# Memory at the border of two loops laid anew, and the backward loop's loads issued by GpSimd

## The chip, the core and the metric

The kernel runs on one core of a Trainium2 chip. A core has five engines that run their own instruction streams: TensorE (PE, matrix products), VectorE (DVE), ScalarE (ACT), GpSimd (POOL) and SyncE (SP), which here only issues transfers. Transfers between device memory (HBM) and the on-chip memory (SBUF), and transposes on the way, are carried out by 16 DMA engines; an instruction on SP or POOL starts them. Results of matrix products land in PSUM. The metric is the device time of one execution in microseconds (us); the time before is 1559.46 us, the median of 3 runs (1558.28 to 1564.76).

## The reference

The program is the forward and the backward pass of one transformer layer with its two branches in parallel, in bf16, for one sequence of S = 2048 rows of D = 448, with 16 heads of 28 and a feed-forward width of 1792:

```python
x  = A_x                                   # [1, 2048, 448]
xn = (x - mean(x)) / sqrt(var(x) + 1e-5)
q, k, v = split(xn @ wqkv)                 # 16 heads, Dh = 28
p   = softmax(q @ k.T * Dh ** -0.5)
mha = concat_heads(p @ v) @ wo
ffn = (silu(xn @ w_gate) * (xn @ w_up)) @ w_down
out = x + mha + ffn
# results: out, and for grad_out (the gradient of out) the gradients of
# x, wqkv, wo, w_gate, w_up, w_down
```

## The kernel before, in words

A head's 28 columns are padded to 32, so four heads make a group of 128 partitions (G = 4 groups, `g`) and two heads a pair (8 pairs, `pr`). The order of instructions on each engine is the order in which the program writes them. There is no planner; waits come from the tiles that the instructions share, and from pools: a tile of a pool with n buffers waits for the readers and writers of the tile n before it, and a pool opened after others are closed waits for whatever was last done in the memory that it gets.

*Prologue (0 to about 60 us).* x is loaded and normalized, the weights of the projections are padded into `wq_sb`, Q, K and V of group 0 are made.

*Forward attention loop (to about 680 us).* It runs over steps (g, qc, kt): 4 groups, 4 blocks of 512 query rows, 16 tiles of 128 keys. A step makes the scores of four heads (L651), their exponentials (L655), and the product with V (L628, `pv`). Between these matmuls PE takes items from a queue: `fill(pace)` pops so many items as the work left, spread over the steps left, allows. The items are the whole feed-forward branch, forward and backward, tile of F by tile of F (`ffn_items`, L432 to L489: its matmuls write to `f_ps`, its temporaries come from the pool `ftmp`), the weight gradients of that branch (`dW_items`, L401: `dwd_sb` and `dw_o` are their output tiles, `dw_o` written by a transpose that SP issues, L425), the projections of the next group, and for each finished block of 512 rows the attention output and its gradient (`o_items`, from L527: tiles `o_raw`, `rlc`, `oT`, `dOl`, `dOT` from the pools `op_` and `op1`). `o_items` stores the gradient in two forms: `spo_d` (rows, L581) and `dOT_d` (transposed, L585), and SP stores the hidden activations and their gradients in `hO_d`, `da_d`, `du_d`. The last items of the loop are those of the last block (`late`): the transposes `tr`, the products `do`, then 16 matmuls and a copy for the gradient of wo (`dwo_items`, L514) and its store to out_3 by four GpSimd instructions (`dwo_out`, L509).

*The border (about 680 to 692 us).* The pools of the forward loop are closed, those of the backward loop opened (`wp` for weights, `ckp` for chunks, `spg` for row forms, `ework` for E, `dwork` for ds, `twin` for dsT). SP issues the loads of Ksp (a transpose), dOsp (from `spo_d`), the four pieces of W_down and two chunks.

*Backward loop (to about 1485 us).* 512 units, each a pair, a block of 512 keys (`kc`), and 128 query rows (`w`, `qi`). A unit makes scores (L959) and the gradient of the probabilities (L969) on PE, E by ScalarE's exponential (L978), and ds by VectorE's multiply (L984). Eight units make a window W (64 windows). A window's ds are needed transposed: three transfers of two units each (dsT, 512 KB, SP, L1011), the last two units by PE and VectorE (L894, L896). From E and ds come the gradients of V and K (`acc_mm`, L868, with dOsp and Qsp), from dsT that of Q (`dq_mm`, L909, with Ksp). `dq_out` (L913) sums the latter on GpSimd over the key blocks; `dkv_sp` and `dq_sp` are transposes of finished gradients which SP issues two or three units later (`sp_later`). Every window also carries one filler job on PE: W 1 to 16 the output rows (`y`, L823: 19 matmuls, with W_down, `wo_pad` and x), later the gradients of wqkv (`dwq`) and dx from da (W 22 to 37) and from du (W 42 to 49 and 54 to 61), 14 or 15 matmuls each (L829). The job of a window takes a chunk `ck` (576 or 448 KB) and often an `x_c` (112 KB), which `job_load` (L736) loads two windows ahead into pools with three buffers. `extra_load` (L711) issues, one a window, the pieces of the next pair (QD and KV, L594 to L600), the rows of the next group (Qsp and Ksp by transposes, dOsp by a load, L602 to L610), the weights W of the next stage (L709) and, in the last two windows, grad_out (`dy`, L728). The results of the jobs leave by GpSimd's stores from `row_o`.

All these loads and transposes of the backward loop are issued by SP, so they share SP's instruction stream and one DMA queue (q1). GpSimd's transfers have another queue (q0). Window 0 calls `job_load(2)` twice: once ahead of the loop, and once as W + 2.

*Final loop (about 1504 us to the end).* 16 row tiles of dx: partial sums and the gradients of Q, K, V times the weights of wqkv (L1037 on), the backward pass of the norm, the store.

Of the kernel before, what the change touches and what calls it, by code (L numbers as in the profile page):

```python
# [38 lines left out]
def kernel(  # L39
# [52 lines left out]

# [7 lines left out]
    wq_sb = bp.tile([P, 4, 3, G, P], BF16, name="wq_sb")  # L100
# [4 lines left out]
    op_ = bst.enter_context(tc.tile_pool(name="op_", bufs=2))  # L105
    op1 = bst.enter_context(tc.tile_pool(name="op1", bufs=1))
# [294 lines left out]
    def dW_items(fc):  # L401

        out = []
        for wi in range(3):
            box = {}

            def go(t, wi=wi, box=box):
# [9 lines left out]
                if wi == 0:  # L417
                    o = fpool["ftmp"].tile([P, D], BF16, name="dwd_sb")
                    dve.tensor_copy(out=o[:], in_=acc[:, :D])
                    pool.dma_start(out=out_6[fc * P:(fc + 1) * P, :], in_=o[:])  # L420
                else:
                    w = dwT[wi - 1]
                    dve.tensor_copy(out=w[:, :D], in_=acc[:, :D])
                    o = fpool["ftmp"].tile([P, 4, P], BF16, name="dw_o")
# [89 lines left out]
    def dwo_items(g):  # L514
        box = {}

        def go(t):
# [3 lines left out]
            if t == NT - 1:  # L521
                o = fpool["ftmp"].tile([P, D], BF16, name="dwd_sb")
                dve.tensor_copy(out=o[:], in_=box["ps"][:, :D])
                dwo_out(g, o)
        return [[(MMD, lambda t=t: go(t)) for t in range(NT)]]

    def o_items(g, qc, o_ps):  # L527

        o_raw = op_.tile([P, 512], FP32, name="o_raw")
# [6 lines left out]
        def tr(i):  # L536
# [8 lines left out]
            rlc = st["rlc"] = op_.tile([P, 4, 4], FP32, name="rlc")  # L545
# [5 lines left out]
            oT = op_.tile([P, 512], BF16, name="oT")  # L551
# [5 lines left out]
        def do(i):  # L557
# [5 lines left out]
            if i < 3:  # L563
# [3 lines left out]
            prod = op1.tile([P, 16, HP], FP32, name="prod")  # L567
            dve.tensor_tensor(out=prod[:], in0=dps,
                              in1=O_sp[g][:, tsl, :].rearrange("p t (h r) -> p (t h) r", r=HP), op=ALU.mult)
            delta = op_.tile([P, 16], FP32, name="delta")  # L570
            dve.tensor_reduce(out=delta[:], in_=prod[:, :, 0:DH], axis=AX.X, op=ALU.add)
            dOl = op_.tile([P, 4, P], BF16, name="dOl")
            dOv = dOl[:].rearrange("p t (h r) -> p (t h) r", r=HP)
            dve.tensor_tensor(out=dOv, in0=dps, in1=rlb.unsqueeze(2).to_broadcast([P, 16, HP]), op=ALU.mult)
            ndl = op_.tile([P, 16], FP32, name="ndl")
            dve.scalar_tensor_tensor(out=ndl[:], in0=delta[:], scalar=-1.0, in1=rlb, op0=ALU.mult, op1=ALU.mult)
            dve.tensor_copy(out=dOv[:, :, 28], in_=ndl[:])
            lo = op_.tile([P, 16], FP32, name="lo")
# [3 lines left out]
            dT = op_.tile([P, 512], BF16, name="dOT")  # L582
# [5 lines left out]
                    + (dwo_items(g) if qc == 3 else []))  # L588


# [3 lines left out]
    def load_pair(pr, pieces=range(4)):  # L594
# [3 lines left out]
        for i in pieces:  # L598
            sp.dma_start(out=qd[pr][i % 2][64 * (i // 2):64 * (i // 2) + 64],
                           in_=(qT_d, kT_d, dOT_d, vT_d)[i][g, r:r + 64, :])  # L600

    def load_rows(g, i):  # L602
# [3 lines left out]
        if i == 2:  # L606
            sp.dma_start(out=t[:].rearrange("p t c -> p (t c)"), in_=spo_d[g])
# [26 lines left out]
    for i, (g, qc, kt) in enumerate(steps):  # L634
# [45 lines left out]
    wp = cst.enter_context(tc.tile_pool(name="wp", bufs=2))  # L680
# [18 lines left out]
    wtile, chunk, dsp, dqacc = {}, {}, {}, {}  # L699

    w_src = {"wd": B_w_down.rearrange("(fc p) d -> p fc d", p=P), "wg": wT_d[0], "wu": wT_d[1], "wq": wqT_d}

    def load_w(nm, pieces=range(4)):
        if 0 in pieces:
            wtile[nm] = wp.tile([P, NFC, D], BF16, name="W")
        for i in pieces:
            sl = slice(4 * i, min(4 * i + 4, 3 * G if nm == "wq" else NFC))
            if sl.start < sl.stop:
                sp.dma_start(out=wtile[nm][:, sl], in_=w_src[nm][:, sl])  # L709
# [14 lines left out]
    def load_dy(i):  # L724

        if i == 0:
            wtile["dy"] = wp.tile([P, NFC, D], BF16, name="W")
        sp.dma_start(out=wtile["dy"][:, 7 * i:7 * i + 7], in_=dy_d[:, 7 * i:7 * i + 7, :])  # L728
# [7 lines left out]
    def job_load(i):  # L736
# [3 lines left out]
        if j[0] == "y":  # L740
            t = ckp.tile([P, NFC + G, P], BF16, name="ck")
            sp.dma_start(out=t[:], in_=hO_d[j[1]])
            x = ckp.tile([P, D], BF16, name="x_c")
            sp.dma_start(out=x[:], in_=x_d[:, j[1], :])
            chunk[i] = (t, x)
        elif j[0] == "dx":
            t = ckp.tile([P, NFC + G, P], BF16, name="ck")
            sp.dma_start(out=t[:, :NFC], in_=(da_d, du_d)[j[1]][j[2]])
# [378 lines left out]
```

## Time and profile before

| what | value |
|---|---|
| runs | 1558.28, 1559.46, 1564.76 us |
| profiled execution | 1558.67 us |
| span of its instructions | 1556.9 us |
| mean granted TensorE clock | 0.965 of full speed |

By stage (busy us of each engine; DMA is the mean busy share of the 16 DMA engines; GB/s is what they moved):

| stage, us | PE | DVE | ACT | POOL | DMA | GB/s |
|---|---|---|---|---|---|---|
| prologue, 0 to 60 | 43.1 | 38.7 | 31.2 | 18.8 | 0.51 | 132 |
| forward, 60 to 640 | 565.7 | 360.1 | 475.4 | 79.0 | 0.70 | 146 |
| end of forward and border, 640 to 691.9 | 40.6 | 15.3 | 26.9 | 10.6 | 0.52 | 126 |
| backward loop, 691.9 to 1484.7 | 727.4 | 680.0 | 589.6 | 165.9 | 1.11 | 209 |
| between the loops, 1484.7 to 1503.6 | 4.8 | 1.3 | 1.9 | 7.7 | 0.86 | 212 |
| final loop, 1503.6 to 1556.9 | 46.5 | 26.3 | 23.3 | 11.4 | 0.49 | 165 |

How the lines of the profile are read. The page gives first each engine's busy time, its share of the span and its instructions, then the span in 40 slices with a digit for each (9: busy 90% or more). Part 4 follows the chain of work that ended last from the end back to the start, and gives shares of the span by engine and line. Part 5 has one row for each group of instructions: line, engine, operation, output <- inputs with partitions x elements and type, count | busy time in us, mean ns of one | idle time of the engine just ahead of them, and the releaser that ended most of it, with its part. A row of stretches is: from:to in us, its length, the busy time and count of the chosen instructions, granted clock, DMA share, GB/s. A row of a timeline is: start, duration in us, engine, line, operation, output <- input, count, and in brackets the idle time before it with what ended it. SPq and POOLq are the streams of SP and GpSimd; the duration of a transfer there is the time that its issue took, not the transfer's. A row of DMA issues gives the count and the median time from issue to landing.

### The profile page before, as it was taken

What the parts mean: (1) busy time and instruction counts of PE and PEld (TensorE: products, weight loads), DVE (VectorE), ACT (ScalarE), POOL (GpSimd) and SP (SyncE); (2) the same over time, 40 slices, a digit from 0 to 9 for tenths busy, and PEclk for the clock granted to TensorE, in tenths of its full rate; (3) what the DMA queues carried; (4) which work ended last, traced back from release to release, by engine and by line L of the source; (5) the groups of instructions that cost most, each with busy time, mean ns of one, the idle gap of its engine ahead of it and who ended that gap; (6) DMA issues with size and microseconds to landing.
All of it is one profiled execution on the core that took longest, in us unless ns stands there. A gap on an engine that the chain in (4) does not pass through costs nothing.

```text
span 1556.9 us, 31518 instructions
## 1 busy us (share of the span) xinstructions
PE 1428.1 (92%) x12278; PEld 577.4 (37%) x12278; DVE 1121.8 (72%) x1459; ACT 1148.4 (74%) x1312; POOL 293.3 (19%) x479
## 2 busy tenths in 40 slices
PE   6899999999999999969989899889898889999968
PEld 3233333333333333323333335333334333533434
DVE  7465656665666666538977789888888888998935
ACT  4678888887888877647767677777777777787824
POOL 4001111111111111110221122212212222221222
PEclk8899999999999999979999999999999999999979
DMA  6566647766777678769999999999999999999984
GB/s 172 111 151 132 145 101 162 144 147 127 156 151 148 140 152 155 153 176 212 230 214 205 217 195 192 218 205 224 205 204 194 205 226 208 189 212 213 185 224 134
DMA packets 764854, 277.69 MB, mean 178 GB/s; under 512 B 730960, under 2 KB 744208, under 8 KB 764704
## 3 DMA queue, kind: packets, MB, share of 16 engines
q1 hardware_dynamic: 748944, 238.90, 79.8%
q0 software_dynamic: 14960, 36.60, 8.8%
q8 instruction: 96, 1.57, 0.4%
q14 instruction: 54, 0.44, 0.1%
q10 hardware_dynamic: 800, 0.17, 0.1%
HBM read 64.15 MB, written 59.24 MB: 79 GB/s over the span
## 4 chain that ended last, share of the span: by engine, by line
PE 65%; DMA 15%; DVE 9%; ACT 6%; issue 4%; SPq 1%; DVEq 0%; POOL 0%; ACTq 0%; POOLq 0%
DMA dsT<-ds 12%; PE s_ps L651 9%; PE f_ps L413 8%; PE f_ps L439 8%; PE sd L959 6%; PE acc L868 5%; ACT E L978 5%; PE o_ps L628 5%; DVE ds L984 4%; PE aux L909 3%; PE sd L969 3%; PE sd L894 3%; PE f_ps L198 3%; PE sd L1043 2%; PE aux L823 2%
## 5 line engine op out<-in xcount | busy, mean ns | idle before, releaser
L984 DVE TENSOR_TENSOR ds<-sd,E 128x1024 bf16<-128x1024 f32 x512 | 607.8, 1220 | 121.7 <-DMA dsT<-ds 48.0
L978 ACT ACTIVATE E<-sd 128x1024 bf16<-128x1024 f32 x512 | 521.0, 1024 | 194.3 <-PE sd L969 125.1
L655 ACT ACTIVATE eT<-s_ps 128x1024 bf16<-128x1024 f32 x512 | 496.5, 1021 | 135.3 <-PE s_ps L651 134.3
L959 PE MATMUL sd<-KV,QD 32*128 32x512 bf16 x1024 | 203.0, 391 | 47.0 <-DVE ds L984 33.0
L969 PE MATMUL sd<-KV,QD 32*128 32x512 bf16 x1024 | 203.7, 390 | 12.9 <-ACT E L978 4.6
L651 PE MATMUL s_ps<-qT,kT 32*128 32x512 bf16 x1024 | 195.9, 391 | 0.5 <-ACT eT L655 0.5
L868 PE MATMUL acc<-E,dOsp 128*32 128x512 bf16 x1024 | 138.5, 394 | 0.1
L868 PE MATMUL acc<-ds,Qsp 128*32 128x512 bf16 x1024 | 138.5, 394 | 0.0
L959 PEld LDWEIGHTS <-QD 32*128 32x128 bf16 x1024 | 57.6, 91 | 208.2 <-issue 194.5
L439 PE MATMUL f_ps<-xnT,wgu 128*128 128x512 bf16 x448 | 119.5, 385 | 9.6 <-DVE w_sb L465 9.6
L829 PE MATMUL aux<-W,ck 128*128 128x448 bf16 x448 | 112.5, 356 | 0.0
L628 PE MATMUL o_ps<-eT,v_sp 128*32 128x512 bf16 x1024 | 103.6, 397 | 4.9 <-DMA v_sp<-vT 4.9
L651 PEld LDWEIGHTS <-kT 32*128 32x128 bf16 x1024 | 47.1, 91 | 161.4 <-issue 157.9
L413 PE MATMUL f_ps<-xn_sp,f_sp 128*128 128x448 bf16 x448 | 98.9, 354 | 0.0
L969 PEld LDWEIGHTS <-QD 32*128 32x128 bf16 x1024 | 69.1, 91 | 64.1 <-issue 60.3
L894 PE MATMUL sd<-ident_bf,ds 128*128 128x128 bf16 x1024 | 70.8, 224 | 15.7 <-DVE ds L984 15.5
L896 DVE COPY dsT<-sd 128x1024 bf16<-128x1024 bf16 x128 | 82.1, 683 | 3.7 <-PE sd L894 3.5
L413 PEld LDWEIGHTS <-f_sp 128*128 128x128 bf16 x672 | 58.9, 98 | 67.0 <-issue 20.5
L909 PE MATMUL aux<-dsT,Ksp 128*32 128x512 bf16 x1024 | 71.8, 400 | 4.8 <-DMA dsT<-ds 4.8
L894 PEld LDWEIGHTS <-ds 128*128 128x128 bf16 x1024 | 62.4, 100 | 30.5 <-issue 30.4
L451 DVE SCALAR_TENSOR_TENSOR g<-t_sb,f_ps 128x512 f32<-128x512 f32 x56 | 38.4, 685 | 43.8 <-ACT t_sb L449 43.8
L925 POOL TENSOR_TENSOR dq_acc<-dq_acc,dq_s 128x512 f32<-128x512 f32 x32 | 40.5, 1265 | 130.5 <-ACT dq_s L921 130.5
(145 smaller groups left out, 1711.3 us busy)
## 6 DMA issues: line engine op xcount, KB each, us to landing
ck<-hO_d SPq DMA_DIRECT2D x17, 576.0 KB, 5.2
hO_d<-hduT SPq DMA_DIRECT2D x56, 128.0 KB, 3.4
da_d<-hduT SPq DMA_DIRECT2D x56, 128.0 KB, 3.1
du_d<-hduT SPq DMA_DIRECT2D x56, 128.0 KB, 3.3
ck<-da_d SPq DMA_DIRECT2D x16, 448.0 KB, 4.3
ck<-du_d SPq DMA_DIRECT2D x16, 448.0 KB, 4.4
dq_c<-dqkv_d SPq DMA_DIRECT2D x8, 768.0 KB, 5.0
dqkv_d<-dkv_o POOLq DMA_DIRECT2D x64, 64.0 KB, 4.1
```

The source lines that it names most:

```text
L413: pe.matmul(acc[:, :D], lhsT=src[:, t, wi, :], rhs=rhs[:, t, :D], start=(t == 0), stop=(t == NT - 1))
L439: pe.matmul(st[name][:], lhsT=w(c), rhs=src[:, tsl, c, :], start=(c == 0), stop=(c == 3))
L628: pe.matmul(o_ps[HP * hh:HP * (hh + 1), :], lhsT=v[:, kt, HP * hh:HP * (hh + 1)], rhs=e[hh // 2][:, hh % 2, :], start=(kt == 0), stop=(kt ...
L651: pe.matmul(s_ps[:, j, :], lhsT=kT[r:r + HP, kt * P:(kt + 1) * P], rhs=qT[r:r + HP, qc * 512:(qc + 1) * 512], start=True, stop=True, tile_ ...
L655: act.activation(out=e[:], in_=s_ps[:], func=ACT.Exp, scale=SCALE)
L868: pe.matmul(acc[r:r + HP, :], lhsT=src[:, qt, 64 * hp + HP * j:64 * hp + HP * j + HP], rhs=m[:, j, :], start=(qt == 0), stop=(qt == NT - 1 ...
L894: pe.transpose(ps[:, u, i, :], ds[:, u, i // 4, (i % 4) * P:(i % 4 + 1) * P], ident_bf[:])
L909: pe.matmul(ps[r:r + HP, :], lhsT=Ks[:, kc * 4 + kt, 64 * hp + HP * j:64 * hp + HP * j + HP], rhs=dsT[:, 4 * s_:4 * s_ + 4, j, kt, :], sta ...
L959: pe.matmul(s_ps[:, j, :], lhsT=q[HP * j:HP * j + HP, qt * P:(qt + 1) * P], rhs=kv[HP * j:HP * j + HP, kc * 512:(kc + 1) * 512], start=Tru ...
L969: pe.matmul(d_ps[:, j, :], lhsT=q[r:r + HP, qt * P:(qt + 1) * P], rhs=kv[r:r + HP, kc * 512:(kc + 1) * 512], start=True, stop=True, tile_p ...
L978: act.activation(out=E[k][:], in_=s_ps[:], func=ACT.Exp, scale=SCALE)
L984: dve.tensor_tensor(out=ds[:, u % 2], in0=d_ps[:], in1=E[u][:], op=ALU.mult)
```

## The change

It has two halves. The first is about memory and the end of the forward loop:

- `wq_sb` moves from the forward loop's pool `bp` into a new pool `wpa`, which stays open; the backward loop's W_down (`wd`), `wu` and `dy` take its place there one after the other, `wg` and `wq` go to another pool, `wpb`.
- The four loads of W_down are issued by SP during the forward loop, in the last block of the last group at kt = 4, 7, 10 and 13.
- The pools `op_` and `op1` and a new one, `fout` (for `dwd_sb` and `dw_o`, which were in `ftmp`), are opened after `ftmp`; in the backward loop `ework` and `dwork` are opened first. E and ds thereby lie on other memory of the forward loop.
- In the last block, 5 of the matmuls for wo's gradient come ahead of `tr` and `do`, the other 11 after them.
- The loads ahead of the backward loop (Ksp, dOsp, chunk 2) are issued inside its first window: dOsp after unit 2, chunk 2 after unit 4, Ksp after unit 6. The second `job_load(2)` is dropped. In the final loop a pool is opened ahead of two others.

The second half: every load of the backward loop that isn't a transpose (`ck`, `x_c`, W, the pieces of QD and KV for pairs 1 to 7, dOsp, `dy`) is issued by GpSimd instead of SP. The transposes (dsT, Qsp, Ksp, `dkv_sp`, `dq_sp`) stay with SP, and so do the pieces of pair 0 and W_down in the forward loop. SP's instructions fall from 847 to 702, GpSimd's rise from 424 to 549; the order of PE's, DVE's and ACT's is otherwise the same.

```diff
@@ prologue @@
+    wpa = ctx.enter_context(tc.tile_pool(name="wpa", bufs=1))
+    wq_sb = wpa.tile([P, NFC, D], BF16, name="W")[:].rearrange("p n d -> p (n d)")[:, :12 * G * P].rearrange(
+        "p (c t g r) -> p c t g r", c=4, t=3, g=G)
-    wq_sb = bp.tile([P, 4, 3, G, P], BF16, name="wq_sb")
-    op_ = bst.enter_context(tc.tile_pool(name="op_", bufs=2))
-    op1 = bst.enter_context(tc.tile_pool(name="op1", bufs=1))
@@ open_ffn @@
-        for nm, n in (("ftmp", 2), ("fT", 2), ("spp", 2)):
+        for nm, n in (("fT", 2), ("spp", 2), ("ftmp", 2), ("fout", 2), ("op_", 2), ("op1", 1)):
@@ dW_items, dwo_items (dwd_sb, dw_o); o_items (its tiles from fpool["op_"], fpool["op1"]) @@
-                    o = fpool["ftmp"].tile([P, D], BF16, name="dwd_sb")
+                    o = fpool["fout"].tile([P, D], BF16, name="dwd_sb")
...
@@ end of o_items @@
+        if g == G - 1 and qc == 3:
+            a, b, w = late.pop()
+            late.append([w[:5], a, b, w[5:]])
@@ load_w, moved ahead of the forward loop @@
+    wtile = {}
+    w_home = {"wd": wpa, "wu": wpa, "dy": wpa}
...
-                sp.dma_start(out=wtile[nm][:, sl], in_=w_src[nm][:, sl])
+                (sp if nm == "wd" else pool).dma_start(out=wtile[nm][:, sl], in_=w_src[nm][:, sl])
@@ load_pair, load_rows @@
-            sp.dma_start(out=qd[pr][i % 2][64 * (i // 2):64 * (i // 2) + 64],
+            (pool if pr else sp).dma_start(out=qd[pr][i % 2][64 * (i // 2):64 * (i // 2) + 64],
...
-            sp.dma_start(out=t[:].rearrange("p t c -> p (t c)"), in_=spo_d[g])
+            pool.dma_start(out=t[:].rearrange("p t c -> p (t c)"), in_=spo_d[g])
@@ forward loop @@
+        if g == G - 1 and qc == 3 and kt in (4, 7, 10, 13):
+            load_w("wd", [(kt - 4) // 3])
@@ pools of the backward loop @@
-    wp = cst.enter_context(tc.tile_pool(name="wp", bufs=2))
+    wpb = cst.enter_context(tc.tile_pool(name="wpb", bufs=1))
...
-    ckp = ast.enter_context(tc.tile_pool(name="ckp", bufs=3))
-    spg_.append(ast.enter_context(tc.tile_pool(name="spg", bufs=2)))
     ework = ast.enter_context(tc.tile_pool(name="ework", bufs=9))
     dwork = ast.enter_context(tc.tile_pool(name="dwork", bufs=5))
+    ckp = ast.enter_context(tc.tile_pool(name="ckp", bufs=3))
     twin = ast.enter_context(tc.tile_pool(name="twin", bufs=2))
+    spg_.append(ast.enter_context(tc.tile_pool(name="spg", bufs=2)))
...
+    w_home["wg"] = w_home["wq"] = wpb
@@ load_dy, job_load (twice so) @@
-        sp.dma_start(out=wtile["dy"][:, 7 * i:7 * i + 7], in_=dy_d[:, 7 * i:7 * i + 7, :])
+        pool.dma_start(out=wtile["dy"][:, 7 * i:7 * i + 7], in_=dy_d[:, 7 * i:7 * i + 7, :])
...
-            sp.dma_start(out=t[:], in_=hO_d[j[1]])
+            pool.dma_start(out=t[:], in_=hO_d[j[1]])
...
-            sp.dma_start(out=x[:], in_=x_d[:, j[1], :])
+            pool.dma_start(out=x[:], in_=x_d[:, j[1], :])
@@ ahead of and in the backward loop @@
-    load_rows(0, 1)
-    load_rows(0, 2)
-    load_w("wd")
     job_load(1)
-    job_load(2)
...
-            if pos == 0:
+            if pos == 0 and W:
                 job_load(W + 2)
...
+        if k == 2:
+            load_rows(0, 2)
+        if k == 4:
+            job_load(2)
+        if k == 6:
+            load_rows(0, 1)
@@ final loop @@
+        one = fin.enter_context(tc.tile_pool(name="one", bufs=1))
         ckf = fin.enter_context(tc.tile_pool(name="ckf", bufs=4))
         wk = fin.enter_context(tc.tile_pool(name="wk", bufs=3))
-        one = fin.enter_context(tc.tile_pool(name="one", bufs=1))
```

More of the change, by code (lines that the diff above doesn't have):

```diff
@@ L423, in go @@
                     dve.tensor_copy(out=w[:, :D], in_=acc[:, :D])
-                    o = fpool["ftmp"].tile([P, 4, P], BF16, name="dw_o")
+                    o = fpool["fout"].tile([P, 4, P], BF16, name="dw_o")
                     sp.dma_start_transpose(out=o[:], in_=w[:])
@@ L521, in go @@
             if t == NT - 1:
-                o = fpool["ftmp"].tile([P, D], BF16, name="dwd_sb")
+                o = fpool["fout"].tile([P, D], BF16, name="dwd_sb")
                 dve.tensor_copy(out=o[:], in_=box["ps"][:, :D])
@@ L581, in do @@
             pool.dma_start(out=spo_d[g, :, 4 * qc * P:(4 * qc + 4) * P], in_=dOl[:].rearrange("p t c -> p (t c)"))
-            dT = op_.tile([P, 512], BF16, name="dOT")
+            dT = fpool["op_"].tile([P, 512], BF16, name="dOT")
             sp.dma_start_transpose(out=dT[:].rearrange("p (t s) -> p t s", t=4),
@@ L588, in o_items, with load_w @@
                     + (dwo_items(g) if qc == 3 else []))
+        if g == G - 1 and qc == 3:
[3 more added lines that the diff above has]
+    w_home = {"wd": wpa, "wu": wpa, "dy": wpa}
+    w_src = {"wd": B_w_down.rearrange("(fc p) d -> p fc d", p=P), "wg": wT_d[0], "wu": wT_d[1], "wq": wqT_d}
+    def load_w(nm, pieces=range(4)):
+        if 0 in pieces:
+            wtile[nm] = w_home[nm].tile([P, NFC, D], BF16, name="W")
+        for i in pieces:
+            sl = slice(4 * i, min(4 * i + 4, 3 * G if nm == "wq" else NFC))
+            if sl.start < sl.stop:
+                (sp if nm == "wd" else pool).dma_start(out=wtile[nm][:, sl], in_=w_src[nm][:, sl])
     NPR = 2 * G
@@ L698 @@
     NW = N // UW
[L699 to L709, printed above, removed]
+    w_home["wg"] = w_home["wq"] = wpb
+    chunk, dsp, dqacc = {}, {}, {}
     def extra_load(W):
```

22 lines of the change are left out of this document (11 added, 11 removed).

## The prediction

> **What bounds the kernel now.** I read the page first (busy shares, slices, chain, groups), then the unit loop in stretches, then SP's timeline in a crowded and in a quiet stretch, the border between the two loops, and the one place where GpSimd already issues loads beside a transpose. The page:
>
> ```profile
> PE 1428.1 (92%) x12278; PEld 577.4 (37%) x12278; DVE 1121.8 (72%) x1459; ACT 1148.4 (74%) x1312; POOL 293.3 (19%) x479
> ...
> DVE  7465656665666666538977789888888888998935
> ...
> DMA  6566647766777678769999999999999999999984
> ...
> PE 65%; DMA 15%; DVE 9%; ACT 6%; issue 4%; SPq 1%; DVEq 0%; POOL 0%; ACTq 0%; POOLq 0%
> DMA dsT<-ds 12%; PE s_ps L651 9%; PE f_ps L413 8%; PE f_ps L439 8%; PE sd L959 6%; PE acc L868 5%; ACT E L978 5%; PE o_ps L628 5%; DVE ds L984 4%; PE aux L909 3%; PE sd L969 3%; PE sd L894 3%; PE f_ps L198 3%; PE sd L1043 2%; PE aux L823 2%
> ...
> L984 DVE TENSOR_TENSOR ds<-sd,E 128x1024 bf16<-128x1024 f32 x512 | 607.8, 1220 | 121.7 <-DMA dsT<-ds 48.0
> ```
>
> From slice 18 on (the backward loop) the DMA digits are all 9 and the chain goes through the dsT transposes: the multiply of L984 waits 48.0 us for them. One row per stretch of that loop, counting L984 alone (us, DVE busy, count); each begins at the first multiply of a window of 8 units:
>
> ```profile
> 703.70:775.80 72.10, 58.06 (x49) 0.99 1.11 222
> 775.80:834.60 58.80, 38.08 (x32) 0.91 1.09 210
> ...
> 1181.90:1299.80 117.90, 85.09 (x74) 0.96 1.14 214
> 1299.80:1402.80 103.00, 85.59 (x73) 1.00 1.11 200
> ```
>
> A window takes 103.0 / 9 = 11.45 us where nothing is late, 72.1 / 6 = 12.0 in the y stage (19 instead of some 15 matmuls of filler), but 58.8 / 4 = 14.7 in windows 7 to 10 and 117.9 / 9 = 13.1 in 39 to 47. With 17 windows at 11.97 and 47 at 11.45 the loop would take 741.6; from the first multiply (691.94) to the end of the last it takes 792.8. So 51 us are lateness, in the stretches where loads are thick. SP's timeline in such a stretch, and in a quiet one:
>
> ```profile
> 881.45 0.53 SPq L742 DMA_DIRECT2D ck<-hO_d  x1
> 882.07 0.38 SPq L744 DMA_DIRECT2D x_c<-in_A_x_dram  x1
> 882.56 3.89 SPq L1011 DMA_TRANSPOSE dsT<-ds  x1
> 886.50 0.57 SPq L709 DMA_DIRECT2D W<-wT_d  x1
> 887.16 3.36 SPq L1011 DMA_TRANSPOSE dsT<-ds  x1
> ```
> ```profile
> 1452.03 10.49 SPq L1011 DMA_TRANSPOSE dsT<-ds  x4
> ```
>
> SP is busy issuing without a rest in the first; a dsT costs it 10.49 / 4 = 2.62 us undisturbed, 3.4 to 3.9 behind a load. The border:
>
> ```profile
> 683.87 0.54 POOL L585 DMA_DIRECT2D dOT_d<-dOT  x1 [3.58 <-DMA dOT<-dOl]
> 684.40 2.03 POOL L512 DMA_DIRECT2D out_dram<-dwd_sb  x4
> ```
> ```profile
> 688.48 2.85 ACT L978 ACTIVATE E<-sd 128x1024 bf16<-128x1024 f32 x3 [15.32 <-DMA dOsp<-spo_d]
> ```
> ```profile
> 691.94 5.75 DVE L984 TENSOR_TENSOR ds<-sd,E 128x1024 bf16<-128x1024 f32 x5 [12.00 <-DMA W<-in_B_w_down_dram]
> ```
>
> The tiles named as releasers are only those that landed near; E and ds lie on the memory of op_ and ftmp, so they wait for the dOT_d store and for the four stores of L512, the last two things the forward loop sends out. Last, the prologue, 14.4 to 24 us, where GpSimd's loads (q0) run beside one transpose:
>
> ```profile
> GB/s 381 303 172 209 205 224 261 373 317 392 373 429 373 355 411 373 355 375 315 450 335 337 360 413 364 260 261 210 159 107 230 235 212 110 114 47 27 0 0 0
> ...
> v_sp<-vT SPq DMA_TRANSPOSE x1, 9.4
> ```
>
> **The change, part by part.**
>
> *Memory at the border.* E and ds no longer lie on anything stored late. The forward loop's last DVE work is the copy of L523 (679.32 + 0.62 = 679.94), the first sd matmul starts at 680.00 and takes 0.39, E takes 1.02: the first multiply can start at about 681.7 instead of 691.94, 10.2 us sooner. What is late next: dOsp. Its tile now lies on the old dwd_sb and its load is GpSimd's, behind the dOT_d store, the four stores (2.03) and the first ck and x_c (about 0.6 each). It may start when the fourth store has landed. Those stores are issued from 684.4 and took about 5 us beside Ksp, dOsp and W; with that traffic gone, 3 (the median of dOT_d stores is 2.7): about 688.5 to 689, plus 5.4 of landing (the dOsp row): 693 to 694. The first acc matmul (L868) wants it 8.2 us after the first multiply (700.2 against 691.9 now), at about 690. PE stops for 3 us, and the multiply with it. Net -7. Bounds: -10 (dOsp in time) and -2 (dOsp as slow as L744's loads there, 7 to 8). I take -7, because the traffic that made those slow is what moves away.
>
> *W_down in forward.* Four SP loads of about 0.6 us of issue, between transposes of dw_o, where SP rests 3 to 8 us at a time; W's new memory (the old wq_sb) has had no reader for tens of us. Cost 0. If the cover fails, dw_o comes 4 us later, and dwT has two buffers filled 5 us apart. The five dwo matmuls put first fill PE's 1.28 us before L539; DVE's chain to 679.94 sets the end, so 0.
>
> *The double load.* One ck and one x_c less (688 KB). The first windows are at their floor anyway: 0.
>
> *125 loads from SP to GpSimd.* 48 ck, 32 x_c, 11 W, 28 pieces of QD and KV, 4 dOsp, 2 dy: 43.4 MB in the loop. SP keeps 192 dsT, 32 dkv_sp, 16 dq_sp and 7 row transposes. SP: from 873.34 to 898.13 it issued 6 dsT, one dkv_sp (1.3) and loads of 1.39 MB without rest, so the loads cost it 24.8 - 6 x 2.62 - 1.3 = 7.8 us, 5.6 us per MB. On GpSimd's queue they can cost the transposes only what they take from the 16 DMA engines. Bounds from below: the prologue's full rate, about 370 GB/s, 2.7 us per MB; its v_sp transpose was held 9.4 - 2.4 (the least v_sp landing) = 7.0 us by 2.4 MB, 2.9 per MB. From above: a later v_sp of 512 KB landed after 12.3 us, where a dsT of that size takes 4.3 at best, beside three GpSimd stores of 512 KB (L225): 8.0 us by 1.6 MB, 5.0 per MB; and at the end of the prologue's window, where small wo_pad loads mix with the transpose, the row reads 107 to 235 GB/s, some 180, 5.6. I take 3.3: ck, W, QD and dOsp (rows of 3.5 to 4.5 KB, into SBUF) are like the dy_sp load, but each ends in a mixed stretch. Demand on the transposes' path per window: 3 x 2.62 + 0.65 (dkv_sp in every second) = 8.5, plus 0.69 MB x 3.3 = 2.3: 10.8, under 11.45. The heaviest stretch, windows 7 to 10: 12 x 2.62 + 4 x 1.3 + 4.3 MB x 3.3 = 50.8 against a floor of 47.9, and Qsp and Ksp (3 us each) just before: 7 late. Of the 51 us I leave 7 in each of three such stretches and 2 more, 23; gain 28. Bounds: 51, and a loss (below). GpSimd: 125 x 0.6 = 75 us more in an engine that is 20% busy. A ck load waits for PE to finish the chunk three back; behind it stand row_o's store, dq_acc and dq_o, and SP's dq_sp waits for dq_o. GpSimd idles 5 to 9 us ahead of dq_o now, against 2 us of new issues: 0, unless that wait passes 5 us. Loads have two windows of slack.
>
> The Trainium skill, page "DMA: Bandwidth & Descriptors", section "Queues, rings and completion order", says that each DMA engine takes turns between its queues, packet by packet. The trace agrees: from 18.5 to 20.0 us q0 ran 118 packets and q1 99. By turns between 4 KB and 256 B a pending load goes nearly first, for the time of its bytes, which is the 2.7 to 2.9.
>
> *The loop's end.* The last dsT goes out at 1487.25, behind a transpose that SP held 5.05 us after the dy load of 1481.37. It leaves up to 5 us sooner; I take 4 (bounds 0 and 5), since the dy load still shares the engines.
>
> **Sum**, from the profiled execution (1558.67; span 1556.9 and 1.8 around it; 0.8 under the median of 1559.46): 1558.7 - 7 - 28 - 4 = 1519.7; predicted 1520.
>
> **The rivals.**
>
> *Nothing gained in the loop.* The DMA digits are 9 throughout, and a byte moved from another queue is still a byte. Then 51 us stay, only the ends gain: 1558.7 - 7 - 4 = 1547.7. Against it: 2.9 beside 5.6 us per MB above, and the quiet windows at 11.45 with the same digit. 17%. The Trainium skill, same page, section "Issuing engines are not separate DMA queues", says just this: issuing from several engines saves only the sequencer's time, usually small. Here that time is 2.62 to 3.9 us per transpose, three per window.
>
> *All of it.* At 2.7 per MB the heaviest stretch needs 48.2 of 47.9: lateness vanishes, and with dOsp in time 1558.7 - 10 - 51 - 5 = 1492.7. 12%.
>
> *Slower: loads starve the transposes.* If a load, by turns, costs the transposes more than its 5.6 us per MB in line, by more than the 11 us of the ends (11 / 43.4 = 0.25 per MB), the kernel is slower; that point is 5.9. At 7.2, 140 GB/s, in the lower part of the prologue's mixed rows, demand rises by 43.4 x 1.6 = 70, nearly all of it late: 1558.7 - 11 + 60 = about 1608. For it: the 12.3 us of v_sp. Against: loads of ck's shape ran at 370. 15%.
>
> **How the numbers follow.** My forecast has 56% (1503 to 1537). The range of 80% reaches past the first rival and nearly to the second: 1496 to 1552. A difference under 0.5% (7.8 us; the three runs before spread 0.4%) can't be told from none. Faster: 56 + 12 and 12 of the first rival's 17, 0.80; the other 5 and 1 of the slower rival's 15 lie within 0.5%: 0.06; slower 0.14.
>
> **What would show it.** Right: the first multiply at about 682; L868 waiting some 3 us for dOsp; windows 7 to 10 at 12 to 14 us and L984's wait for dsT under 25 us; a dsT holding SP 2 to 3 us in all stretches, SP with rests; the final loop starting 15 us or so after the last multiply, not 19. Wrong: dsT landing over 6 us in the median although alone on its queue (starved), or E, dq_o or acc waiting on GpSimd.

## The result, and the profile after

The changed kernel is slower: its median is 1596.45 us (1581.70 to 1629.58, 4 runs) against 1562.11 for the kernel before, a ratio of 1.013 with a 95% interval of 1.010 to 1.017. Its executions spread widely, and the ratio counts only those within 1.5% of the fastest, two of the four; the profiled execution, 1581.70 us with a span of 1579.9, is that fastest one, and why the others are slower is part of what follows. In the traces SP issues 719 transfers instead of 846 and GpSimd 436 instead of 311 (125 moved, and the second chunk 2 dropped, a `ck` and an `x_c`); the counts 847 and 702 given for SP with the change are not those of the traces.

The page of the kernel after (busy shares, slices of the span, chain, the group of the multiply, which is now L987):

```profile
PE 1438.5 (91%) x12278; PEld 580.7 (37%) x12278; DVE 1121.7 (71%) x1459; ACT 1148.8 (73%) x1312; POOL 360.3 (23%) x604
...
DVE  7465656665666666458856888789889789898925
...
DMA  5566648676767678689999999999999999999984
...
PE 64%; DMA 18%; ACT 7%; DVE 7%; issue 3%; SPq 1%; DVEq 0%; POOL 0%; ACTq 0%; POOLq 0%
DMA dsT<-ds 16%; PE s_ps L667 9%; PE f_ps L412 8%; PE f_ps L438 8%; PE sd L962 6%; ACT E L981 5%; PE acc L875 5%; PE o_ps L642 5%; PE sd L972 3%; PE aux L916 3%; PE f_ps L197 3%; DVE ds L987 3%; PE aux L830 3%; PE sd L1052 2%; PE sd L901 2%
...
L987 DVE TENSOR_TENSOR ds<-sd,E 128x1024 bf16<-128x1024 f32 x512 | 608.5, 1220 | 141.4 <-DMA dsT<-ds 69.8
```

DVE and ACT do the same work for the same time as before, PE's same work is 10 us longer; GpSimd is 67 us busier, with the 125 issues it took over. The transposes' share of the chain rose from 12% to 16%, and the multiply's wait for them from 48.0 to 69.8 us. The stretches of the loop (us, DVE busy, count, granted clock, DMA share, GB/s; each begins at the first multiply of a window: window 0, 1 to 6, 7 to 10, 11 to 40, 41, 42 to 63):

```profile
683.20:702.50 19.30, 9.43 (x8) 0.50 0.90 215
702.50:778.40 75.90, 57.80 (x48) 0.97 1.15 210
778.40:853.70 75.30, 38.07 (x34) 0.84 1.19 174
853.70:1223.40 369.70, 285.12 (x240) 0.97 1.13 207
1223.40:1242.40 19.00, 9.41 (x9) 0.92 1.18 203
1242.40:1508.00 265.60, 208.64 (x177) 0.99 1.12 199
```

Window 0 takes 19.3 us instead of 11.7, windows 7 to 10 take 75.3 instead of 58.8, window 41 takes 19.0 instead of 13.6. In windows 7 to 10 the DMA share is the highest of all, 1.19, and the GB/s the lowest, 174: the DMA engines are occupied and move little.

Where the 23.0 us between the two profiled executions are:

| from, to | before, us | after, us | difference |
|---|---|---|---|
| start to the end of the forward loop's last copy (`dwd_sb`) | 679.94 | 681.59 | +1.65 |
| from there to the first multiply | 12.00 | 1.66 | -10.34 |
| windows 0 and 1 | 23.94 | 31.57 | +7.62 |
| windows 2 to 63 | 768.85 | 793.14 | +24.29 |
| last multiply to the end | 72.16 | 71.96 | -0.19 |

At the border, GpSimd's timeline and, from the list of PE's waits, the longest one (engine, line, releaser: us, times, longest):

```profile
685.28 0.54 POOL L584 DMA_DIRECT2D dOT_d<-dOT  x1 [3.33 <-DMA dOT<-dOl]
685.82 2.03 POOL L511 DMA_DIRECT2D out_dram<-dwd_sb  x4
687.88 0.55 POOL L749 DMA_DIRECT2D ck<-hO_d  x1
688.42 0.56 POOL L751 DMA_DIRECT2D x_c<-in_A_x_dram  x1
691.87 0.54 POOL L621 DMA_DIRECT2D dOsp<-spo_d  x1 [2.89 <-PE sd L962]
```
```profile
PE acc L875 <- DMA dOsp<-spo_d: 7.3, 1, 7.3
```

The multiply starts 10 us sooner, as forecast, and then PE stands still for dOsp: its load goes out 0.7 us after the last of the four stores has landed (691.14) and itself lands at 699.41.

The slow stretch inside windows 9 and 10, as SP's timeline and as the transfers of 831 to 839 us (40 slices of 0.2 us):

```profile
821.01 9.04 SPq L1014 DMA_TRANSPOSE dsT<-ds  x2
830.09 1.66 SPq L939 DMA_TRANSPOSE dq_sp<-dq_o  x1
831.80 17.29 SPq L1014 DMA_TRANSPOSE dsT<-ds  x3
```
```profile
DMA  9979999999999999932390099934445992100698
GB/s 64 59 58 65 142 138 133 111 119 140 131 175 109 92 99 127 192 46 38 78 23 1 23 65 173 96 29 31 28 33 25 29 90 22 24 0 24 55 104 174
...
q1 hardware_dynamic: 614, 0.16, 66.2%
q0 software_dynamic: 124, 0.45, 49.8%
...
dsT<-ds SPq DMA_TRANSPOSE x1, 15.2
```

For 8 us the 16 engines move 79 GB/s between them, where transposes alone run at 290 (the kernel before, 794 to 795 us) and loads nearly alone at 370 (its prologue, 18.5 to 20 us), and a dsT lands 15.2 us after its issue. Behind the landing times stand the single packets. In the same kernel, at 797.6 us, ten of the 54 that begin within 0.24 us, the long ones picked out; 30 of the 54 are transposes' packets of 18 ns (start; queue; bytes; ns; end):

```
797.604 q1  256  207  797.811
797.615 q1  256  189  797.804
797.656 q0 4608  178  797.834
797.656 q0 4608  178  797.834
797.683 q0 4608  178  797.861
797.800 q1  256  372  798.172
797.804 q1  256  180  797.984
797.807 q1  256  188  797.995
797.820 q1  256  361  798.181
797.844 q0 4608  178  798.022
```

Most of the transposes' packets of 256 B take 18 ns. Between 793 and 801 us 18% of them take 180 ns or more, between 831 and 839 us 37%, over the whole loop of the kernel before 0.6%. Their times are not spread evenly: from 793 to 801 us nearly all the long ones took 160 to 220 or 340 to 400 ns, one or two times the 178 of a load's packet, and they end together in clumps (797.81, 797.99, 798.18). So they wait for load packets, which is argued from these lengths; the trace doesn't say on which of the 16 engines a packet ran, so whether a transpose's packet waits for a load's on its own engine or on another one isn't shown. Load packets are held up as well: 26 of the 128 between 793 and 801 us took more than 1 us.

Two counts of such stretches are used below. One is the number of dsT (of 192) that landed more than 12 us after their issue: 0 before, 10 after. The other is the number of stretches of at least 3 us in the loop (from 12 us after the first multiply on) in which every slice of 1 us has packets of a transpose and, on another queue, packets of 512 B or more, and moves under 130 GB/s: none before, 8 after, 38 us together, at 731, 793 to 807, 825 to 839, 972 and 1241 us; five of the eight lie in windows 7 to 10. Moving the slices by quarters of a microsecond changes these counts by three at most, and those of the kernel before and of the border half not at all.

### The profile page after: what moved, and what is told of

Same layout as the page of the kernel before. It is cut to its first block, busy times and chain, and to the rows that moved or that the text cites. A ratio compares the mean times of both kernels' runs of the same rounds, so it can differ in the third digit from the quotient of the medians.

```text
span 1579.9 us, 31459 instructions
## 1 busy us (share of the span) xinstructions
PE 1438.5 (91%) x12278; PEld 580.7 (37%) x12278; DVE 1121.7 (71%) x1459; ACT 1148.8 (73%) x1312; POOL 360.3 (23%) x604
## 3 DMA queue, kind: packets, MB, share of 16 engines
q1 hardware_dynamic: 730912, 194.76, 70.3%
## 4 chain that ended last, share of the span: by engine, by line
PE 64%; DMA 18%; ACT 7%; DVE 7%; issue 3%; SPq 1%; DVEq 0%; POOL 0%; ACTq 0%; POOLq 0%
DMA dsT<-ds 16%; PE s_ps L667 9%; PE f_ps L412 8%; PE f_ps L438 8%; PE sd L962 6%; ACT E L981 5%; PE acc L875 5%; PE o_ps L642 5%; PE sd L972 3%; PE aux L916 3%; PE f_ps L197 3%; DVE ds L987 3%; PE aux L830 3%; PE sd L1052 2%; PE sd L901 2%
## 5 line engine op out<-in xcount | busy, mean ns | idle before, releaser
L987 DVE TENSOR_TENSOR ds<-sd,E 128x1024 bf16<-128x1024 f32 x512 | 608.5, 1220 | 141.4 <-DMA dsT<-ds 69.8
L962 PE MATMUL sd<-KV,QD 32*128 32x512 bf16 x1024 | 205.2, 396 | 56.2 <-DVE ds L987 49.0
L972 PE MATMUL sd<-KV,QD 32*128 32x512 bf16 x1024 | 205.8, 394 | 11.0 <-ACT E L981 4.1
L901 PEld LDWEIGHTS <-ds 128*128 128x128 bf16 x1024 | 64.3, 102 | 31.6 <-issue 27.8
```

The source lines that it names most:

```text
L901: pe.transpose(ps[:, u, i, :], ds[:, u, i // 4, (i % 4) * P:(i % 4 + 1) * P], ident_bf[:])
L962: pe.matmul(s_ps[:, j, :], lhsT=q[HP * j:HP * j + HP, qt * P:(qt + 1) * P], rhs=kv[HP * j:HP * j + HP, kc * 512:(kc + 1) * 512], start=Tru ...
L972: pe.matmul(d_ps[:, j, :], lhsT=q[r:r + HP, qt * P:(qt + 1) * P], rhs=kv[r:r + HP, kc * 512:(kc + 1) * 512], start=True, stop=True, tile_p ...
L987: dve.tensor_tensor(out=ds[:, u % 2], in0=d_ps[:], in1=E[u][:], op=ALU.mult)
```

## The experiments

Ratios are to the kernel before, measured beside each kernel on the same chip, with 95% intervals. The last two columns are of the one profiled execution. For the kernel with its stores on ScalarE the record has no ratio, only its four times.

| kernel | ratio | profiled, us | dsT over 12 us | slow stretches |
|---|---|---|---|---|
| before | 1 | 1558.7 | 0 | 0 |
| after | 1.013 (1.010 to 1.017) | 1581.7 | 10 | 8, 38 us |
| border half alone, loads on SP | 1.003 (1.000 to 1.006) | 1568.7 | 0 | 0 |
| loads on GpSimd alone | 1.017 (1.010 to 1.024) | 1591.0 | 11 | 7, 42 us |
| ck and x_c on GpSimd | 1.011 (1.007 to 1.015) | 1566.6 | 1 | 0 |
| the same, profiled again | - | 1587.4 | 4 | 4, 28 us |
| the other loads on GpSimd | 0.998 (0.994 to 1.002) | 1553.8 | 1 | 2, 9 us |
| after, stores on ScalarE | - | 1624.4 | 13 | 8, 39 us |
| after, loads on ScalarE | 0.996 (0.992 to 1.000) | 1544.7 | 2 | 0 |
| ck on GpSimd in pieces | 1.022 (1.017 to 1.027) | 1594.8 | 4 | 4, 13 us |
| before, stores on SP | 1.031 (1.025 to 1.036) | 1602.7 | 0 | 0 |
| border half, 25.7 MB not loaded | 0.963 (0.959 to 0.966) | 1500.3 | 0 | 0 |
| loads on ScalarE, dOsp mended | 0.998 (0.994 to 1.003) | 1561.4 | 2 | 1, 4 us |
| other loads on ScalarE, ck on SP | 0.994 (0.991 to 0.997) | 1554.0 | 0 | 3, 14 us |

**The two halves.** Theory Q: the loads on GpSimd's queue are the loss. Theory B: the border is.

```diff
# border half alone: every load of the backward loop back on SP
-            pool.dma_start(out=t[:], in_=hO_d[j[1]])
+            sp.dma_start(out=t[:], in_=hO_d[j[1]])
# (and so for x_c, da_d and du_d, W, QD and KV, dOsp, dy)
```

> The first half of the change alone: memory at the border, W_down in forward, the double load dropped; all loads of the backward loop issued by SP as before. If the loads on GpSimd's queue are the loss (theory Q), this is at or below before: the first multiply 8 us sooner (683 instead of 692), of which the wait for dOsp and SP's own wait for the four out_3 stores give back 4 to 8: -4 to 0 us against before, and windows 7 to 10 at 59 us as before. If the new memory or the order at the border is the loss (theory B), it is slower than before by 10 us or more.

> The kernel before with only the 125 loads of the backward loop moved to GpSimd. Theory Q (two queues at once cost the transposes more than one): slower than before by 20 to 30 us, windows 7 to 10 at 70 us or more instead of 59. Theory B: no slower than before.

The border half alone came out at 1.003, 1563.3 us in the median of 10 runs, so B's 10 us aren't there; but neither are the 0 to 4 us that Q had it gain. Its first multiply too starts 1.7 us after the last copy, window 0 takes 15.2 us instead of 11.7, and PE waits 3.2 us for dOsp. From the last copy to the end of window 1 it takes 29.6 us, 6.3 less than before. What eats this isn't settled: in this one profile the forward loop ended 11.8 us later than before (691.77 against 679.94), while in the ten other profiles with the same forward loop it ended at 676.9 to 681.9.

The 125 loads alone, on the kernel before, cost 1.017. Q holds: the loss came with the loads. One number went against it: windows 7 to 10 took 59.0 us there, not 70; its slow stretches lay elsewhere (window 24 took 22.2 us, window 46 took 26.4).

**Which loads.**

```diff
# ck and x_c alone on GpSimd: the other loads back on SP
-            (pool if pr else sp).dma_start(out=qd[pr][i % 2][...], ...)
+            (sp if pr else sp).dma_start(out=qd[pr][i % 2][...], ...)
# (and so for W, dOsp, dy; the other kernel does the reverse)
```

> The changed kernel with only the chunks ck and x_c (27 of the 43 MB) on GpSimd; W, QD, KV, dOsp and dy back on SP. If the loss goes with the bytes on GpSimd's queue (Q by bytes), about 0.6 of the difference between the changed kernel and the first half alone remains, 12 to 18 us. If it comes only where chunks and extra pieces pile up on GpSimd (theory P), under 5 us remain.

> The other part: W, QD, KV, dOsp and dy on GpSimd (16 MB), ck and x_c back on SP. Q by bytes: about 0.4 of the difference remains, 8 to 12 us. P: under 5 us; the sum of this and the run with the chunks alone then falls well short of the whole.

The chunks alone carry it: 1.011 against the 1.003 of the border half in the same comparison, some 12 us; the other loads cost nothing, 0.998, rather gain a little. So it doesn't go by bytes (27.8 and 15.6 MB would share the loss 0.6 to 0.4), and theory P, under 5 us, falls too, though the intervals of the chunk kernel and the border half almost touch. Nor does a slow stretch need a chunk: in the changed kernel's at 731 and 1241 us the packets beside the transposes' are of QD and KV pieces alone. But the profile of the chunk kernel was of its fastest execution and showed no slow stretch. A second look was to tell whether such stretches make the long executions:

> A second profile of the kernel with ck and x_c alone on GpSimd. Its profiled execution (1566.6) was the fastest of ten with a median of 1581, and had no slow stretch of 3 us or longer. If those stretches make the difference, an execution of 1575 or more has at least two of them, and one near 1567 none.

It took 1587.4 us, with four stretches, 28 us together: 21 us more than the first profile, with the same code, and all of that in windows 2 to 63 (796.4 and 774.6 us). The worst, 1212 to 1232 us (40 slices of 0.5 us), where window 41 took 29.8 us:

```profile
GB/s 289 472 213 136 36 109 109 23 179 41 90 112 47 160 62 69 27 114 77 41 147 93 43 146 27 60 90 76 46 159 149 353 318 263 83 191 54 52 67 61
...
ck<-du_d POOLq DMA_DIRECT2D x1, 448.0 KB, 15.5
...
dsT<-ds SPq DMA_TRANSPOSE x2, 20.5
```

**Which queue.** Theory T: a load on any queue but the transposes' own takes turns with them. Theory S: it is GpSimd's queue.

```diff
# loads on ScalarE (chunks from the fourth on, W, QD and KV, dOsp from group 1 on, dy)
-            pool.dma_start(out=t[:], in_=hO_d[j[1]])
+            (act if i > 3 else pool).dma_start(out=t[:], in_=hO_d[j[1]])
```

> The changed kernel with its loads issued by ScalarE instead of GpSimd (from the fourth chunk and the second group on; the first three chunks and the first dOsp stay on GpSimd). ScalarE's queue is a hardware queue like SP's. Theory T (a load on any queue other than the transposes' takes turns with them on every engine, and a transpose that works across all 16 engines waits for each of these turns): as slow as the changed kernel, 15 us or more above the first half alone (1563). Theory S (it is GpSimd's software queue that does it): within 6 us of 1563, a few us of them ScalarE's issue time.

S holds by the time: 0.996 of before, 1558.9 us in the median of 10. Most chunks are loaded at the same point: 35 of 44 on GpSimd and 36 of 44 on ScalarE between the ends of the sixth and the seventh multiply of a window, the other nine spread over earlier units on GpSimd, the other eight just ahead of that point on ScalarE. Apart from the first three chunks and the first dOsp, which stay on GpSimd, the queue is what differs. The profile shows two dsT over 12 us, one of them in window 0 beside those first loads, and no slow stretch; but it is the fastest of the ten (1544.7), so it can't say how many the others have. In its page the loads are on q10, and DMA's share of the chain is 8% instead of 18%:

```profile
q1 hardware_dynamic: 730912, 194.76, 69.5%
q10 hardware_dynamic: 17536, 40.96, 9.9%
q0 software_dynamic: 15680, 39.24, 9.6%
...
PE 70%; DVE 9%; DMA 8%; ACT 8%; issue 3%; SPq 1%; ACTq 1%; DVEq 0%; POOL 0%
...
L987 DVE TENSOR_TENSOR ds<-sd,E 128x1024 bf16<-128x1024 f32 x512 | 610.7, 1220 | 111.7 <-PE sd L972 72.4
```

Its windows 7 to 10:

```profile
777.60:830.80 53.20, 38.50 (x33) 0.97 1.14 230
```

53.2 us at 230 GB/s, where the changed kernel took 75.3 at 174, and the kernel before 58.8 at 210. The next kernel asks whether loads and stores must meet on GpSimd's queue:

```diff
# after, with the stores of the backward loop issued by ScalarE (also row_o, dq_o)
-                pool.dma_start(
+                act.dma_start(
                     out=dqkv_d[2 * kc:2 * kc + 2, ...], ...)
```

> The changed kernel with the other traffic of GpSimd's queue in the backward loop (row_o, and dqkv_d from dkv_o and dq_o) issued by ScalarE, so that GpSimd's queue carries the loads alone. If the slow stretches (one load packet at a time, all transposes waiting) need loads and stores together on GpSimd's queue, they go: within 6 us of 1563. If loads on that queue do it by themselves: 1578 or more as in the changed kernel, with three or more such stretches of 3 us and longer.

No: with hardly anything but the loads on it (16 stores of the gradient of wqkv stay) there were 13 late dsT and 8 slow stretches in the profiled execution (1624.4 us), and the four took 1588 to 1627 us.

**What the bytes cost.**

```diff
# border half, with the chunks of the first three jobs used again by the later ones
+        if i > 3 and j[0] in ("y", "dx"):
+            t, x = chunk[1 + i % 3]
+            chunk[i] = (t, None if j[:2] == ("dx", 0) else x)
+            return
```

> The first half alone (1563), leaving out the loads of ck and x_c after the first three jobs: the later jobs multiply these three chunks again, so out and dx come out of the wrong data, and 25 MB are not loaded. It gives the price of these loads in line. At the 5.6 us per MB of the prediction nearly all of the 51 us of lateness would go, 1515 to 1525; if in line they cost little, 1545 to 1560, and then no queue could have won much.

Without these 25.7 MB (counted again) the loop stands near its floor: 746.2 us from the first multiply to the end of the last, where 741.6 was worked out. The stretch of the loop, for the border half and for this kernel, and this kernel's group of the multiply with all its releasers:

```profile
693.44:1494.54 801.10, 606.67 (x512) 0.97 1.10 208
...
678.57:1424.73 746.16, 610.49 (x512) 0.99 1.04 188
...
L991 DVE TENSOR_TENSOR ds<-sd,E 128x1024 bf16<-128x1024 f32 x512 | 610.5, 1220 | 66.8 <-PE sd L976 51.0 <-ACT dkv_o L885 3.3 <-DMA dsT<-ds 2.5
```

The wait for dsT is down to 2.5 us. By the ratios these loads cost (1.0032 - 0.9627) x 1560 = 63 us in line, 2.5 us per MB, and on GpSimd's queue (1.0106 - 0.9627) x 1560 = 75, 2.9 per MB, as a mean over executions with and without slow stretches. By the two profiles the loop alone differs by 54.9 us, 2.1 us per MB; another 14.9 lie in the forward loop (691.77 and 676.90), whose code is the same. So nearly all the lateness of the loop is the price of the chunks, at 2.1 to 2.5 us per MB in line.

```diff
# before, with the stores of the backward loop on SP (also dq_o; row_o two units later)
-                pool.dma_start(
+                sp.dma_start(
                     out=dqkv_d[2 * kc:2 * kc + 2, ...], ...)
```

> The kernel before, with the stores of its backward loop (row_o, and dqkv_d from dkv_o and dq_o; 160 transfers, 13 MB) moved from GpSimd to SP, so that one queue carries nearly everything. T: the turns that the kernel before has too (23 slices of 1 us with packets of both queues and little moved) go, 8 to 15 us faster than before, unless SP's 160 more issues of about 0.5 us make it late. If bytes in line with the transposes are what costs, at the 5.6 us per MB of the prediction: 30 to 70 us slower.

1.031, 48 us slower for 11.8 MB in 144 transfers (the expectation's 13 and 160 were rough), 4 us per MB: the rival's side, and T's gain isn't there. Whether the bytes cost this or SP's 144 more issues, the run doesn't separate. No dsT is late; that the table has no slow stretch for it says little, because the count asks for packets of another queue, and there are next to none. Counted on any queue there is one, of 3 us.

```diff
# ck on GpSimd, cut in pieces of four blocks (x_c uncut)
-            pool.dma_start(out=t[:], in_=hO_d[j[1]])
+            for c_ in range(0, NFC + G, 4):
+                pool.dma_start(out=t[:, c_:min(c_ + 4, NFC + G)], in_=hO_d[j[1]][:, c_:min(c_ + 4, NFC + G)])
```

> The kernel with only ck and x_c on GpSimd (1581), each ck load cut into pieces of at most four of its 14 or 18 blocks, so that a packet is at most 1 KB instead of 4.6 or 7.2 KB. T, where what a turn costs is the length of the load's packet (some 45 ns instead of 178 to 275): at least half of the 18 us over the first half alone goes, 1572 or less. If the bytes count: 1581 as before. If the number of turns counts: slower, 1590 or more.

It didn't test what it was for: in the trace GpSimd's queue carries 7362 packets of 4096 B in the loop (1476 with ck uncut), four rows of 1 KB in one, so the packets never were small. It shows only that four or five transfers in place of one cost more (1.022 against 1.011).

**A better kernel.** dOsp was mended first, on top of the loads on ScalarE:

```diff
     spg_.append(ast.enter_context(tc.tile_pool(name="spg", bufs=2)))
     dqa = ast.enter_context(tc.tile_pool(name="dqa", bufs=1))
+    spg_.append(ast.enter_context(tc.tile_pool(name="dop", bufs=2)))   # dOsp's own pool
...
+    load_rows(0, 2)
     job_load(1)
...
-        if k == 2:
-            load_rows(0, 2)
```

> The kernel with its loads on ScalarE (1559, 0.996 of before), and the border mended: dOsp has a pool of its own over the memory of op_, so that it no longer waits for the four stores to out_3, and it is issued ahead of the first chunk. If dOsp is what fills window 0 (20.3 us there instead of 11.7), it starts at about 688 instead of 692, PE waits 2 to 3 us for it instead of 8, and the kernel takes 1551 to 1554. If the first transposes are late beside those loads anyway, window 0 stays at 18 or more and the time at 1557 to 1560.

Window 0 fell from 20.3 to 15.2 us, with dOsp issued at 688.3, and PE's wait from 8.3 to 3.2. The whole shows none of it, and the 1551 to 1554 us didn't come: 0.998, with an interval that holds its twin's 0.996. So dOsp's late start is a cause of window 0's length, and that it is worth 5 us of the whole is not shown.

```diff
# the other loads on ScalarE, ck and x_c back on SP
-            (pool if pr else sp).dma_start(out=qd[pr][i % 2][...], ...)
+            (act if pr else sp).dma_start(out=qd[pr][i % 2][...], ...)
```

> The twin of the run with only the extra loads on GpSimd (0.998 of before, two slow stretches of 4 and 6 us in its profile): W, QD, KV, dOsp from the second group on and dy now on ScalarE's queue, ck and x_c on SP as there. If ScalarE's queue has none of GpSimd's slow stretches, no stretch of 3 us or longer, and 0.990 to 0.997 of before. If the slow stretches weren't what held the twin back, the same 0.998.

0.994 (0.991 to 0.997), 1550.0 us in the median of 12: faster than both kernels, than the kernel before by 0.6%. Of the 4.7 us between its profile and that of the kernel before, 3.1 lie at the border with windows 0 and 1, 1.5 in the windows behind them and 1.8 at the end, less 1.7 in the forward loop; so the loads themselves gained little. Its profile has three stretches of 4 to 6 us all the same, and the packets beside the transposes' in them are on ScalarE's queue (q10), though no dsT lands after more than 12 us. So that queue isn't free of slow stretches; how many it has on average one profile can't say.

## Why the prediction was wrong

- *The border's memory: right, and used up sooner than forecast.* The first multiply was forecast at 681.7 and came at 683.25, with the forward loop 1.65 later: 10.3 us sooner against the last copy, as worked out. The term that failed is dOsp's landing. It was put at 693 to 694 from stores that take 3 us and a load that takes 5.4, "because the traffic that made those slow is what moves away". The last two stores took 3.9 and 3.8, the load 7.5, landing at 699.41, and PE waited 7.3 us instead of 3: what moved away was replaced by dsT and by three chunks which GpSimd issues at the same time. Net -2.7 (with windows 0 and 1) instead of -7. That dOsp waits for these stores was right: in every kernel with the new border it goes out 0.3 to 0.8 us after the last of them has landed, and with a pool of its own it goes out without waiting (688.33). Which part of the old memory holds it back no trace shows. With dOsp's load on SP, in the border half, PE waited the 3.2 us that were forecast.
- *125 loads from SP to GpSimd: the step that failed.* It was to gain 28 us and lost 24 (windows 2 to 63); the multiply's wait for dsT, which was to fall, rose from 48.0 to 69.8 us. The step set 3.3 us per MB on GpSimd, taken from loads which ran almost alone, against 5.6 in line, and two things are wrong in it. First, the 5.6 was read off SP's busy time, and that isn't the sum of what the single loads cost: with 120 fewer issues in the loop SP still spent 769 of 825 us in issuing, after 751 of 793, and a dsT's issue simply lasted longer. The chunks' price in line, measured by leaving them out, is 2.1 to 2.5 per MB. The 3.3 was near as a mean (2.9 for the chunks), but against 2.1 to 2.5 there is nothing to gain. Second, the price beside transposes isn't a constant. Most loads land little later (ck on GpSimd after 6.0 us in the median, against 4.5 on SP before); but there are stretches in which loads and transposes together move 58 to 110 GB/s, and a dsT lands after 12 to 20 us. The upper row of the bound, v_sp after 12.3 us beside three stores, and the rows of 107 to 235 GB/s in the prologue pointed that way; I had them in hand and gave them the lesser weight.
- *The sign of being wrong.* The prediction named a dsT landing after more than 6 us in the median, and it came: 6.5 instead of 5.7. But with the loads on ScalarE the median is 6.6 and the time 0.996, so the median doesn't tell the two apart; the late ones do, 10 against 2.
- *The rule of turns.* The Trainium skill, page "DMA: Bandwidth & Descriptors", section "Queues, rings and completion order", has each engine take turns between its queues by packets. The long packets above, one or two times as long as a load's, fit such turns. But by the rule alone, each engine by itself, a pending load costs the time of its own bytes, and the prediction's 2.7 to 2.9 followed. Between 831 and 839 us 0.45 MB went over q0 and 0.16 MB over q1; at the 370 and 290 GB/s of each alone that is 1.8 us of work, an estimate, and it took 8. So the rule doesn't cover what happened there.
- *Several issuing engines.* The Trainium skill, same page, section "Issuing engines are not separate DMA queues", was the better guide: from ScalarE the same loads gain 0.4%, which agrees with its "usually small". That they lose 1.3% from GpSimd it doesn't say.
- *The rivals.* The one whose direction came true is "loads starve the transposes", 15%, at 1608 us, 49 more than before. The comparison's 1.013 is 21 us more, less than half of that. Its sign, v_sp's 12.3 us, was right; its prices, 7.2 per MB against 5.6, were both far from the measured (2.9 for the chunks on GpSimd, 2.1 to 2.5 in line), so that the median of 1596 comes near its 1608 is luck. "Nothing gained", 1547.7, is near the loads on ScalarE (0.996 of 1559.5, 1553).
- *The double load and W_down in forward:* nothing in the runs stands against their 0, and none tests them alone. With W_down in it the forward loop ended at 676.9 to 691.8 us in eleven profiles, in the middle at 681.5; without, at 679.9 to 683.1 in three.
- *The loop's end:* -4 was forecast, -0.2 came. The last dsT goes out 2.2 us after the end of the last multiply (1510.18 and 1507.96), as it did before (2.5: 1487.25 and 1484.74), so taking the dy load off SP didn't bring it forward. With dy on ScalarE the last multiply's end is 70.3 to 71.1 us from the end of the whole, against 72.2 before.
- *GpSimd's time:* 75 us more were forecast, 67 came, and GpSimd has 0% of the chain.

What stays open: why the same loads, most of them issued at the same point of a window, bring such stretches often from GpSimd's queue and seldom from ScalarE's, why the other loads on GpSimd do little harm by themselves, and how far counts from single profiles hold for other executions. The length of the packets isn't the answer in windows 7 to 10: there a chunk goes in packets of 4608 B on either queue, and the stretches are on GpSimd's alone. Later chunks differ (7168 B on q0, two rows in one, and 3584 on ScalarE's queue); the kernel meant to test the length couldn't make the packets short, and with 4096 B the stretches were there.

## What to carry to other kernels

Where one queue carries DMA transposes that set the pace, price a load on another queue by the worst row in which the two overlap, not by the load's rate alone, and look at several executions: a loss that comes in rare stretches of 3 to 13 us can be missing from the fastest one. The busy time of an issuing engine that never rests doesn't give the price of its instructions; leave the loads out once to see what they cost. Before giving an engine's loads to GpSimd, try ScalarE's queue; here all of them there gave 0.996, and those that aren't issued every window 0.994.

## What the runs showed of the hardware that was not expected

- Beside transposes, loads on GpSimd's queue can come to stretches in which all 16 DMA engines together move little: 84 GB/s for 13 us (1214 to 1227 us in the second profile of the chunk kernel). Of the transposes' 256 B packets, which mostly take 18 ns, 15 to 37% then take 180 ns or more, about one or two times as long as a load's packet: 160 to 220 and 340 to 400 ns beside load packets of 178 (the changed kernel, 793 to 801 us), 260 to 340 and 500 to 600 beside load packets of 272 and more (the second profile of the chunk kernel).
- The same loads on ScalarE's queue, most of them issued at the same point of the window, gave 0.996 instead of 1.013.
- GpSimd's queue packs rows: 7168 B packets of two rows of 3584, 4480 B of five rows of 896, and 4096 B of four rows of 1 KB, where SP's and ScalarE's queues carry rows of 3584 and 896 B one to a packet.
